# SyncE's list times set to those of a trace, and the stores of the split output weights given a later place

## The chip, the cores and the metric

The kernel runs on 1 core of one Trainium2 chip. The metric is the device time of one execution in microseconds. Three runs of the kernel before gave 1342.36, 1343.71 and 1345.11 us, median 1343.71.

## The reference

An attention without softmax feeds two feed-forward layers. B = 8 batches, H = 8 heads, S = 576 rows, D = 64, so 4608 tokens of 512 columns.

```python
kv = einsum('bhsd,bhse->bhde', k, v)
out = einsum('bhsd,bhde->bhse', q, kv)
out = out / sqrt(mean(out * out, axis=-1) + 1e-6) * g_norm
x = out.transpose(0, 2, 1, 3).reshape(4608, 512)
h = max(max(x @ w1, x @ w2), x @ w3)          # 512 -> 768
x = h @ w_out                                 # 768 -> 512
h = x @ w_in                                  # 512 -> 2048
g = s * relu(h)**2 + b
return g @ moe2_w_out                         # 2048 -> 512
```

## The kernel before

**Tiling.** The tokens are worked in nine blocks of 512. Blocks 0 to 7 are the first 512 rows of each batch; block 8 collects the 64 remaining rows of all batches. Weights and activations are split into a high and a low part, and a product is three matmuls (lines 183 to 185: high by high, high by low, low by high).

**Stages.** The first stage (every job whose position lies below CUT) does, in one stream: the attention of all batches (`load_kv`, `load_rem`, `load_q`, `q_turn`, `kv_mm`, `o_mm`, the norm in `o_sq`, `msc_mm`, `rsqrt_c`, `u_hi`, `u_both`, `wide_bc`, `normed`); the unpacking and splitting of the weights w1, w2, w3 (chunks w0 to w17) and w_out (chunks o0 to o5), in `plan_conv`; and the first layer of blocks 0, 1 and 2 by the plain way (`g1_part`, `g2_mm`). Later stages work the other blocks by a Strassen-like scheme with seven products in place of eight, and then the second layer.

**What goes through memory.** Normed attention outputs are stored to `xd` (`x_out`, lines 537 and 539). The results of the first layer's second product are copied out of PSUM on ScalarE (`g2_out`, L612) into a ring of two tiles (tag "st") and stored to `x1d` (`x1_store`, L615), by ScalarE's own DMA queue for blocks 0 and 1. The third copy of a block therefore waits until the first store has landed. A block's second product fills all four PSUM banks of the tag "g"; two of them then take the broadcast of a norm (`wide_bc`, L490), and the next block's `g1_part` waits for the bank of the third copy. The split output weights `W_o0` to `W_o5` (512 KB each) are stored to `od` (`wo_out`, L337) and come back only at the start of a later stage (`wo_back`, L1508, 530 to 549 us), because their slots are used for other things in between.

**Order.** No order is written out by hand. Each piece of work is a job with a position, an engine, a cost in us, what it reads and writes, and a lag from its end to when its result may be used. `arrange` (lines 73 to 153) plays these through and issues each engine's instructions in the order that comes out. At each step it takes the engine that can begin earliest and, of the jobs that are ready there, the first by position:

```python
begin, eng = min((max(free.get(e, 0.0), min(when(n) for n in h)), e) for e, h in heaps.items() if h)
n = min(m for m in heaps[eng] if when(m) <= begin)
```

So a cost shifts when later jobs count as ready, on every engine, and with it the order of the instructions; for jobs marked "DVE/ACT" it also decides which of the two engines takes them. A tag with so many slots makes a new tile's job wait for the last use of an old one. The chip then runs each engine's stream in that order with semaphores. Positions count in steps of one `g1` group; a block is SL = 22 of them, block 0 begins at 0, and CUT is 59.

**SyncE's jobs in the first stage.** Loads of k, v (one pair of heads at a time, two DMAs of 256 KB), of the remaining rows of k and v (two of 128 KB), of q (four DMAs of 288 KB into the one tile `qraw`, whose next load waits for the last `q_turn` of the one before), of the raw weights (512 KB), and the stores to `xd`, `od` and `wd`. The raw chunk o5 (and o4) is loaded into a slot that the unpacking of w14 (and w15) uses first; the first raw chunk of the second layer's weights (p0) goes into the tile "craw", which the unpacking of o4 uses last.

Of the kernel before, what the change touches and what calls it, by code (L numbers as in the profile page):

```python
# [30 lines left out]
def attention_max_ffn_relu2_ffn(ctx: ExitStack, tc, q, k, v, g_norm, w1, w2, w3, wo, wi, w2o, s, b, out):  # L31
# [14 lines left out]
    B, H, S, D = q.shape  # L46
# [13 lines left out]
    SL = G1 + KD  # L60
# [7 lines left out]
    def job(pos, eng, cost, fn, *args, r=(), w=(), a=(), lag=None):  # L68
        jobs.append((pos, len(jobs), eng, cost, fn, list(args), r, w, a, lag or (2.0 if eng == "SP" else 0.1)))
# [143 lines left out]
    od = dram.tile([P, M1, 2, N], F32, name="od")  # L213
# [99 lines left out]
    def stage(tag, name, shape, dtype):  # L313
        return lambda: (at_ if tag[0] == "c" else base).tile(shape, dtype, tag=tag, name=name, bufs=SIZE.get(tag, 1))
# [226 lines left out]
    def plan_x_out(bb, p, pos, o):  # L541
        if bb == B or p % 2:
            u = p if bb == B else p // 2
            job(pos, "SP", 1.1 if bb == B else 1.95, x_out, bb, u, r=o if bb == B else [f"o{bb}.{u}:0", f"o{bb}.{u}:1"],
                w=[f"xd{bb}:{c}" for c in ([2 * (p % 2) + p // 2] if bb == B else (u, 2 + u))])

    def x_tiles(j):
# [71 lines left out]
    def plan_conv(kk, src, pos, load, a, pr, slot=None, store=None):  # L619
        key = (kk[0], int(kk[1:]))  # L620
        raw, tr = f"raw_{kk}", f"tr_{kk}"
        ra, tra = stage(a, raw, [P, 4 * N], U16), stage(pr, tr, [P, 2, N], I32)
        gc = f"gc_{kk}"
        own = kk[0] != "p"
        gca = stage("cgc", gc, [P, N], U16) if own else lambda: st["tr", key][:, 1].bitcast(U16)[:, :N]
        job(load, "SP", 1.95, conv_load, key, src, ra, w=[raw], a=[(a, raw)], lag=6.0 if kk[0] == "p" else 2.0)
        job(pos, "DVE/ACT", (0.43, 0.66), conv_c, key, gca, None if own else tra, r=[raw], w=[gc if own else tr + ":r"],
            a=[("cgc", gc) if own else (pr, tr)])
        job(pos, "ACT", 0.71, conv_t, key, tra if own else None, r=[gc if own else tr + ":r"], w=[tr + ":t"], a=[(pr, tr)] if own else [])
        job(pos, "DVE/ACT", (0.43, 0.72), conv_r, key, r=[raw], w=[tr + ":r"])  # L630
        job(pos, "DVE", 0.69, conv_s, key, r=[raw], w=[tr + ":r"])
        job(pos, "DVE", 0.69, conv_sum, key, r=[tr + ":r"], w=[tr + ":t"])
        if store is None:
            job(pos, "ACT", 0.63, conv_hi, key, slot, r=[tr + ":t"], w=[f"W_{kk}:0"], a=[(slot, f"W_{kk}")])
            job(pos, "DVE", 0.69, conv_lo, key, r=[tr + ":t", f"W_{kk}:0"], w=[f"W_{kk}:1"])
        else:
            job(store, "SP", 1.1, conv_store, key, r=[tr + ":t"], w=[f"wd{key[1] // 4}:{key[1] % 4}"], lag=5 if pos < CUT else None)

    def plan_kv(bb, load, mm, n):
        lag = 2.0 if bb < 2 else 8.0  # L640
        job(load(0) + 0.01 if bb < 3 else mm(0) - WA + 0.1, "SP", 1.1, load_rem, bb, w=["rem"], lag=lag)
        for p in range(NP):
            job(load(p), "SP", 2.1, load_kv, bb, p, w=[f"k{bb}.{p}", f"v{bb}.{p}"],
                a=[("k", f"k{bb}.{p}"), ("v", f"v{bb}.{p}")], lag=lag)
            job(mm(p), "PE", 0.65, kv_mm, bb, p, r=[f"k{bb}.{p}", f"v{bb}.{p}", "rem"], w=[f"kvp:{p}"])
        for p in range(0, NP, n):
            job(mm(p + n - 1) + 0.01, "ACT", 0.4, kv_out, bb, p, n, r=[f"kvp:{i}" for i in range(p, p + n)],
                w=[f"kvc{bb}:{i}" for i in range(p, p + n)], a=[("kvc", f"kvc{bb}")] if p == 0 else [])
# [9 lines left out]
                w=[f"qh{bb}.{p // 2}:{p}"], a=[(HS[p // 2] if p < NP else "kvc", f"qh{bb}.{p // 2}")] if p % 2 == 0 else [])  # L658

    def plan_q(bb, p, n, pos):  # L660
        job(pos, "SP", 2.1 * n, load_q, bb, p, n, w=[f"qraw{bb}:{i}" for i in range(p, p + n)],
            a=[("qraw", f"qraw{bb}")] if p == 0 else [])

    def plan_o(bb, u, pp, turn, mm):
# [42 lines left out]
    def plan_wide(bb, t, f, sq):  # L707
        o = [[f"or{p}:{b_}" for b_ in range(B)] if bb == B else [f"o{bb}.{p // 2}:{p % 2}"] for p in range(NP)]
        ms, y, uc, uh, ul = (f"{c}c{bb}" for c in ("ms", "y", "u", "uh", "ul"))
        for p in range(NP):  # L710
            src, r = (lambda p=p: st["ops", p // 2][:, p % 2]), [f"ops{bb}.{p // 2}:{i}" for i in (p // 2 * 2, p // 2 * 2 + 1)]
            if bb == B:
                src, r = (lambda p=p: rest[0][:, p]), o[p]
            job(sq(p), "ACT", 0.59, lambda p=p, src=src: o_sq(bb, p, src()), r=r, w=[f"sq{bb}.{p}"], a=[(SQ[p], f"sq{bb}.{p}")])
        job(t, "PE", 1.1, msc_mm, bb, 0, NP, r=[f"sq{bb}.{p}" for p in range(NP)], w=[ms], a=[("ms", ms)])
        for i in range(5):
            job(t + f * (0.3 + 0.1 * i), "DVE" if i > 2 else "ACT", 0.7 if i > 2 else 0.65, rsqrt_c, bb, 0, NP, i,
                r=[[ms], [y], [y], [ms], [y]][i], w=[[y], [y], [uc], [uc], [uc]][i], a=[("y", y), ("u", uc)] if i == 0 else [])
        job(t + 0.9 * f, "DVE", 0.42, u_hi, bb, r=[uc], w=[uh], a=[("y", uh)])
        job(t + 1.0 * f, "DVE", 0.69, u_both, bb, r=[uc, uh], w=[ul], a=[("xb", ul)])  # L720
        b = [f"bc{bb}.0:0", f"bc{bb}.0:1", f"bc{bb}.1:0", f"bc{bb}.1x:0"]
        job(t + 1.3 * f, "PE", 0.52, wide_bc, bb, r=[ul], w=b, a=[("ops", f"bc{bb}.0"), ("*g", f"bc{bb}.1"), ("*g", f"bc{bb}.1x")])
        for k, p in enumerate((2, 3, 0, 1)):
            job(t + f * (1.6 + 0.05 * k), "DVE", 0.7, normed, bb, p, r=[b[p], "g_sb"], w=o[p])
            if bb == 1:
                plan_x(bb, p, 20 + 0.1 * p, o[p], "DVE", p == 0)
        for p in range(NP) if bb > 1 else ():
            plan_x_out(bb, p, t + f * (1.9 + 0.3 * (p // 2 * 2)), o[p])
# [41 lines left out]

    plan_q_rows(0, lambda p: Z - 0.5 + 0.1 * p, lambda p: Z - 0.1 + 0.02 * p if p < NP else Z - 0.12)
    plan_kv(0, lambda p: Z + p, lambda p: Z + p + 0.5, 1)
    job(Z + 2.45, "SP", 1.0, load_scalars, w=["scalars"])
    job(Z + 2.45, "DVE", 0.15, scale_g, r=["scalars"], w=["g_sb"])
# [10 lines left out]
    for n in range(G1):  # L785
        plan_conv(f"w{n}", w1_src(n), WS_ * n - 3 if n > 3 else Z + CP + n, WS_ * n - 5 if n > 3 else Z + LP[n], W1S[n], sets[n % 4], slot=W1S[n])
    for m in range(M1):
        plan_conv(f"o{m}", [(0, P, W16[3][m * P:(m + 1) * P, :])], WO_ + 0.8 * m, WO_ - 2 + 0.8 * m,
                  WOS[m], sets[m % 2], slot=WOS[m])

    for bb in range(1, B + 1):
# [9 lines left out]
        for u in range(NP // 2):  # L801
            a, f = (t + 6 * FA * u, FA) if bb > 1 else (A1 + AS * u, 1)
# [27 lines left out]
                    plan_g2(j, n, t + G1 + 0.3 + m * (0.5 if j == 0 else 0.66) + 0.01 * n, [m])  # L830
            plan_g2_out(j, n, t + G1 + (max(n + 1.01, 2.01 + 0.1 * n) if 0 < j < ND - 1 else 3 + 0.3 * n if j == 0 else 3.7 + 0.05 * n))
    for m in range(M1):
        job(SL + 6 + 3 * m, "SP", 1.95, wo_out, m, r=[f"W_o{m}:0", f"W_o{m}:1"], w=[f"od:{m}"])

# [673 lines left out]
    def plan_pairs():  # L1510
# [35 lines left out]
        for n in range(2 * M2):  # L1546
            if n < PA:
                pos, raw, pr = SL + 14 + (CUT - SL - 21) / PA * n, "craw", "ctr"
            elif n < PB:
                pos, raw, pr = TB + 28 + (TC - TB - 28 - 12) / (PB - PA) * (n - PA), *(("o2", "o3"), ("o4", "o5"))[n % 2]  # L1550
            else:
                pos, raw, pr = TC + 2 + 1.3 * (n - PB), *(("v0", "v1"), ("v2", "v3"))[n % 2]
            plan_conv(f"p{n}", p2_src(n), pos, pos - 3, raw, pr, store=pos + 1.5)
# [15 lines left out]
    for n, qq in enumerate(PAIRS):  # L1569
        for g in range(4):  # L1570
            for i in range(7):
                G = 4 * n + g
                pos = T2 + 7 * G + i
# [66 lines left out]
```

## Time and profile before

| | us |
|---|---|
| median of the runs | 1343.71 |
| the profiled execution, its own time | 1345.25 |
| its span | 1343.4 |
| TensorE (PE) busy | 1323.7 |
| VectorE (DVE) busy | 972.7 |
| ScalarE (ACT) busy | 765.3 |
| DMA queue of SyncE and its share of the 16 engines' span | 259.74 MB, 62.4% |
| share of PE in the chain that ended last | 95% |

The times are of one execution. Busy time leaves out DMA-issuing and semaphore instructions. The granted clock of TensorE is 0.998 of full speed over the span. A timeline row gives start, duration, engine, line, operation and output<-input; the bracket is the idle time of that engine ahead of it and what ended it. "SPq" and "ACTq" are the instructions by which SyncE and ScalarE issue DMAs.

### The profile page before, as it was taken

Reading aid. Unit: us, or ns where it says so; the run is one execution under the profiler, and the core shown is the slowest. Engines: PE = TensorE matmul, PEld = TensorE weight load, DVE = VectorE, ACT = ScalarE, POOL = GpSimd, SP = SyncE. Lnnn points to the kernel's source line nnn. Section 1 sums busy time; section 2 is a strip of 40 time slices with the busy share of each in tenths; the row PEclk is TensorE's granted clock in tenths of the full one; section 3 lists DMA queues with packets and bytes.
Section 4 is the critical chain, followed back from the end, with each engine's and each line's share of the span. In section 5 each row is a group of like instructions: output and inputs, shape, how many; then the busy total and the mean of one; then the engine's idle time right before and its main releaser. Section 6 shows DMA issues by size and latency. Waiting matters only on the chain.

```text
span 1343.4 us, 19629 instructions
## 1 busy us (share of the span) xinstructions
PE 1323.7 (99%) x6910; PEld 1083.4 (81%) x6910; DVE 972.7 (72%) x1677; ACT 765.3 (57%) x1360; POOL 16.9 (1%) x20
## 2 busy tenths in 40 slices
PE   7999998999999999999999999999999999999998
PEld 5776766788888888888888889888888888888888
DVE  5995455688977766665657668658888888888886
ACT  6874443464454643454656567567775757566565
POOL 0000100100000000000000000000000000000000
PEclk9999999999999999999999999999999999999999
DMA  9999998375458688775535655436584464453541
GB/s 279 292 193 255 222 220 189 123 248 206 180 195 254 189 256 275 250 245 184 180 142 189 233 184 176 167 134 224 195 310 149 145 206 151 162 176 123 188 125 59
DMA packets 245987, 264.41 MB, mean 197 GB/s; under 512 B 119680, under 2 KB 178560, under 8 KB 243712
## 3 DMA queue, kind: packets, MB, share of 16 engines
q1 hardware_dynamic: 244000, 259.74, 62.4%
q10 hardware_dynamic: 1888, 3.41, 0.8%
q8 instruction: 54, 0.88, 0.3%
q14 instruction: 45, 0.37, 0.1%
HBM read 159.29 MB, written 103.81 MB: 196 GB/s over the span
## 4 chain that ended last, share of the span: by engine, by line
PE 95%; DMA 2%; ACT 1%; SPq 1%; DVE 1%; issue 0%; ACTq 0%; DVEq 0%
PE ps_a L1015 15%; PE zs_a L1169 15%; PE fp_a L1444 11%; PE zs_b L1169 7%; PE ps_b L1015 7%; PE g L183 7%; PE g L185 7%; PE g L184 7%; PE fp_b L1444 5%; PE zs_c L1169 4%; PE ps_c L1015 4%; PE fp_c L1444 3%; PE kvor L382 1%; PE ops L451 1%; DMA x1d<-x 1%; PE msc L497 1%
## 5 line engine op out<-in xcount | busy, mean ns | idle before, releaser
L324 ACT ACTIVATE zx<-z 128x512 fp32r<-128x512 f32 (+1 forms) x280 | 158.5, 586 | 119.6 <-PE zs_a L1169 39.1
L1169 PE MATMUL zs_a<-zx,w_q 128*128 128x512 f32 (+1 forms) x960 | 211.0, 368 | 0.1
L327 DVE TENSOR_TENSOR zx<-z,zx 128x512 fp32r<-128x512 f32 (+1 forms) x280 | 171.7, 634 | 53.4 <-ACT zx L324 50.1
L1015 PE MATMUL ps_a<-x_q,w_q 128*128 128x512 f32 (+1 forms) x960 | 206.0, 368 | 0.0
L1169 PEld LDWEIGHTS zs_a<-zx,w_q 128*128 128x128 f32 x960 | 168.2, 188 | 30.3 <-DVE zx L327 0.3
L1015 PEld LDWEIGHTS ps_a<-x_q,w_q 128*128 128x128 f32 x960 | 167.8, 189 | 29.9
L1169 PE MATMUL zs_b<-zx,w_q 128*128 128x512 f32 (+1 forms) x480 | 108.6, 368 | 0.0
L1015 PE MATMUL ps_b<-x_q,w_q 128*128 128x512 f32 (+1 forms) x480 | 105.1, 368 | 0.0
L1169 PEld LDWEIGHTS zs_b<-zx,w_q 128*128 128x128 f32 x480 | 84.7, 189 | 15.1
L1015 PEld LDWEIGHTS ps_b<-x_q,w_q 128*128 128x128 f32 x480 | 84.2, 189 | 15.0
L183 PE MATMUL g<-xh,w_w 128*128 128x512 f32 x216 | 87.7, 406 | 2.8 <-ACT x L612 2.4
L185 PE MATMUL g<-xh,w_w 128*128 128x512 f32 x216 | 84.7, 392 | 0.7 <-DVE w_w L327 0.7
L184 PE MATMUL g<-xl,w_w 128*128 128x512 f32 x216 | 84.7, 392 | 0.2 <-DVE xl L327 0.2
L1452 ACT ACTIVATE fc<-fp_a 128x512 f32<-128x512 f32 x54 | 32.1, 596 | 69.3 <-PE fp_a L1444 63.7
L1044 ACT ACTIVATE cs<-cs 128x512 f32<-128x512 f32 (+1 forms) x60 | 35.1, 585 | 54.9 <-DVE cs L871 54.2
L1031 ACT ACTIVATE cs<-ps_a 128x512 f32<-128x512 f32 (+1 forms) x80 | 43.4, 554 | 26.1 <-PE ps_a L1015 22.3
L871 DVE TENSOR_TENSOR cs<-ps_b,cs 128x512 f32<-128x512 f32 (+1 forms) x40 | 24.9, 637 | 44.1 <-issue 32.9
L184 PE MATMUL g<-h,wo 128*128 128x512 f32 x144 | 56.1, 390 | 0.0
L185 PE MATMUL g<-h,wo 128*128 128x512 f32 x144 | 56.0, 389 | 0.0
L183 PE MATMUL g<-h,wo 128*128 128x512 f32 x144 | 56.0, 389 | 0.0
L183 PEld LDWEIGHTS g<-xh,w_w 128*128 128x128 f32 x216 | 40.5, 188 | 18.4 <-issue 5.6
L1169 PE MATMUL zs_c<-zx,w_q 128*128 128x512 f32 (+1 forms) x240 | 54.5, 368 | 0.0
(382 smaller groups left out, 2510.0 us busy)
## 6 DMA issues: line engine op xcount, KB each, us to landing
z<-gd SPq DMA_DIRECT2D x64, 512.0 KB
gd<-cs SPq DMA_DIRECT2D x96, 256.0 KB
fs<-sd SPq DMA_DIRECT2D x24, 512.0 KB
z<-gd SPq DMA_DIRECT2D x48, 256.0 KB
sd<-fs SPq DMA_DIRECT2D x18, 512.0 KB
hd<-fh SPq DMA_DIRECT2D x36, 256.0 KB
fhl<-hd SPq DMA_DIRECT2D x36, 256.0 KB
raw_w<-in_moe_w_dram SPq DMA_DIRECT2D x18, 511.0 KB
```

Source lines behind the costliest of these rows:

```text
L183: nc.tensor.matmul(ps, lhsT=w[:, 0, sl], rhs=xh, start=first, stop=False)
L184: nc.tensor.matmul(ps, lhsT=w[:, 0, sl], rhs=xl, start=False, stop=False)
L185: nc.tensor.matmul(ps, lhsT=w[:, 1, sl], rhs=xh, start=False, stop=last)
L324: act(out=out, in_=src, func=AF.Copy)
L327: eng.tensor_tensor(out=out, in0=src, in1=hi.bitcast(F32), op=ALU.subtract)
L871: eng.tensor_tensor(out=out, in0=in0, in1=in1, op=op)
L1015: nc.tensor.matmul(ps, lhsT=w[:, a, c], rhs=x[:, b_], start=new and k == 0 and e == 0, stop=k == HK - 1 and e == 2, skip_group_check=True)
L1031: act(out=st["cs", G, i, m], in_=st["ps", G, BANK[i], m][:, :n], func=AF.Copy)
L1044: act(out=h, in_=st["ps", G, BANK[i], m][:, :width(q)] if i == 6 else h, func=AF.Relu)
L1169: nc.tensor.matmul(ps, lhsT=w[:, a, c], rhs=x[:, b_], start=new and k_ == 0 and e == 0, stop=k_ == 3 and e == 2, skip_group_check=True)
L1444: nc.tensor.matmul(ps, lhsT=w[:, u, c], rhs=x[:, v_], start=new and k == 0 and e == 0, stop=k == HK - 1 and e == 2, skip_group_check=True)
L1452: act(out=st["fc", a, G, i], in_=ps, func=AF.Copy)
```

## The change

Seven numbers change, all of them positions or costs that `arrange` reads; no instruction is added or taken away, and no other line is touched.

```diff
     def plan_x_out(bb, p, pos, o):
-            job(pos, "SP", 1.1 if bb == B else 1.95, x_out, ...
+            job(pos, "SP", 0.75 if bb == B else 1.4, x_out, ...
...
     def plan_conv(kk, src, pos, load, a, pr, slot=None, store=None):
-        job(load, "SP", 1.95, conv_load, ...
+        job(load, "SP", 1.95 if kk[0] == "p" else 1.75, conv_load, ...
...
     def plan_kv(bb, load, mm, n):
-            job(load(p), "SP", 2.1, load_kv, ...
+            job(load(p), "SP", 1.75, load_kv, ...
...
     def plan_q(bb, p, n, pos):
-        job(pos, "SP", 2.1 * n, load_q, ...
+        job(pos, "SP", 2.95 * n, load_q, ...
...
     for m in range(M1):
-        job(SL + 6 + 3 * m, "SP", 1.95, wo_out, m, ...
+        job(2 * SL + 4 + 1.8 * m, "SP", 1.4, wo_out, m, ...
```

With n = 4, the list's time of a load of q goes from 8.4 to 11.8 us. The six stores of the split output weights go from the positions 28, 31, 34, 37, 40, 43 to 48, 49.8, 51.6, 53.4, 55.2, 57; block 2 spans the positions 44 to 66.

## Rows read from the trace of the kernel before

**Rows 1.** Page, view 1: busy us (share of the span) and number of instructions.
```profile
PE 1323.7 (99%) x6910; PEld 1083.4 (81%) x6910; DVE 972.7 (72%) x1677; ACT 765.3 (57%) x1360; POOL 16.9 (1%) x20
```
**Rows 2.** Stretches: length, busy us (x) of PE, PEld, DVE, ACT, POOL, clock, DMA share, GB/s.
```profile
40.00:50.00 10.00, 10.00 (x62) 8.07 (x61) 9.27 (x16) 5.34 (x10) 0.00 (x0) 1.00 1.24 230
...
100.00:110.00 10.00, 9.63 (x119) 7.56 (x121) 2.72 (x4) 2.39 (x4) 0.00 (x0) 1.00 0.93 342
...
200.00:210.00 10.00, 5.50 (x24) 3.55 (x22) 5.72 (x9) 1.19 (x2) 0.00 (x0) 0.97 1.03 351
```
**Rows 3.** The same view, first and last of seven stretches from 280 to 1330 us.
```profile
280.00:400.00 120.00, 120.00 (x531) 99.38 (x530) 102.06 (x181) 62.27 (x106) 0.00 (x0) 1.00 0.55 196
...
1200.00:1330.00 130.00, 129.93 (x710) 113.32 (x709) 108.46 (x208) 82.87 (x167) 0.67 (x2) 1.00 0.41 133
```
**Rows 4.** Waits of PE over the span: total us, times, longest us.
```profile
PE bc L490 <- DVE ul L482: 2.7, 2, 2.1
PE g L183 <- ACT x L612: 2.4, 1, 2.4
```
**Rows 5.** Waits of PE from 100 to 135 us.
```profile
PE bc L490 <- DVE ul L482: 0.7, 1, 0.7
...
PE g L183 <- ACT xh L324: 0.4, 1, 0.4
PE g L184 <- DVE xl L327: 0.2, 1, 0.2
```
**Rows 6.** Timeline of SyncE's issues, 58 to 108 us.
```profile
58.83 0.38 SPq L370 DMA_DIRECT2D v<-in_v_dram  x1
71.22 2.84 SPq L271 DMA_DIRECT2D raw_o<-in_moe_w_out_dram  x2
...
96.88 0.89 SPq L337 DMA_DIRECT2D od<-w_o  x2
...
98.50 1.00 SPq L337 DMA_DIRECT2D od<-w_o  x1
107.03 0.38 SPq L370 DMA_DIRECT2D k<-in_k_dram  x1
```
**Rows 7.** Timeline of SyncE's issues, 126 to 221 us.
```profile
126.41 0.47 SPq L337 DMA_DIRECT2D od<-w_o  x1
...
220.13 3.51 SPq L337 DMA_DIRECT2D od<-w_o  x1
```
**Rows 8.** Chain that ended last, 103 to 111 us: start us, us, what.
```profile
103.89 4.07 DMA x1d<-x
...
108.05 0.61 ACT x L612
...
110.11 0.64 ACT xh L324
```
**Rows 9.** The same chain, 197 to 208 us.
```profile
197.30 4.01 DMA k<-in_k_dram
...
201.39 6.30 DMA x1d<-x
```
**Rows 10.** Timeline of DVE and ACT, 95 to 208 us.
```profile
95.88 0.68 DVE L327 TENSOR_TENSOR w_o<-tr_o,w_o 128x512 fp32r<-128x512 f32 x1
...
128.39 0.78 DVE L438 STREAM_TRANSPOSE qt<-qraw 128x576 f32<-128x576 f32 x1 [2.50 <-DMA qraw<-in_q_dram]
...
199.21 0.78 DVE L438 STREAM_TRANSPOSE qt<-qraw 128x576 f32<-128x576 f32 x1 [6.91 <-DMA qraw<-in_q_dram]
...
207.67 0.60 ACT L612 ACTIVATE x<-g 128x512 f32<-128x512 f32 x1 [11.27 <-DMA x1d<-x]
```
**Rows 11.** Stretches of 2 to 6 us: columns as in rows 2.
```profile
65.00:71.00 6.00, 6.00 (x28) 4.98 (x27) 6.00 (x11) 5.99 (x11) 0.00 (x0) 1.00 0.32 111
...
104.00:106.00 2.00, 2.00 (x13) 1.41 (x11) 0.00 (x0) 0.60 (x1) 0.00 (x0) 1.00 1.05 418
...
208.00:210.00 2.00, 1.68 (x6) 1.18 (x6) 0.00 (x0) 0.87 (x2) 0.00 (x0) 0.84 1.05 404
210.00:212.00 2.00, 2.00 (x9) 0.55 (x12) 0.00 (x0) 0.00 (x0) 0.00 (x0) 0.50 0.95 337
212.00:214.00 2.00, 2.00 (x60) 1.79 (x54) 1.40 (x3) 1.61 (x3) 0.00 (x0) 0.81 0.08 32
```

More of the change, by code (lines that the diff above doesn't have):

```diff
@@ L543, in plan_x_out @@
             u = p if bb == B else p // 2
-            job(pos, "SP", 1.1 if bb == B else 1.95, x_out, bb, u, r=o if bb == B else [f"o{bb}.{u}:0", f"o{bb}.{u}:1"],
+            job(pos, "SP", 0.75 if bb == B else 1.4, x_out, bb, u, r=o if bb == B else [f"o{bb}.{u}:0", f"o{bb}.{u}:1"],
                 w=[f"xd{bb}:{c}" for c in ([2 * (p % 2) + p // 2] if bb == B else (u, 2 + u))])
@@ L625, in plan_conv @@
         gca = stage("cgc", gc, [P, N], U16) if own else lambda: st["tr", key][:, 1].bitcast(U16)[:, :N]
-        job(load, "SP", 1.95, conv_load, key, src, ra, w=[raw], a=[(a, raw)], lag=6.0 if kk[0] == "p" else 2.0)
+        job(load, "SP", 1.95 if kk[0] == "p" else 1.75, conv_load, key, src, ra, w=[raw], a=[(a, raw)], lag=6.0 if kk[0] == "p" else 2.0)
         job(pos, "DVE/ACT", (0.43, 0.66), conv_c, key, gca, None if own else tra, r=[raw], w=[gc if own else tr + ":r"],
@@ L642, in plan_kv @@
         for p in range(NP):
-            job(load(p), "SP", 2.1, load_kv, bb, p, w=[f"k{bb}.{p}", f"v{bb}.{p}"],
+            job(load(p), "SP", 1.75, load_kv, bb, p, w=[f"k{bb}.{p}", f"v{bb}.{p}"],
                 a=[("k", f"k{bb}.{p}"), ("v", f"v{bb}.{p}")], lag=lag)
@@ L660, in plan_q @@
     def plan_q(bb, p, n, pos):
-        job(pos, "SP", 2.1 * n, load_q, bb, p, n, w=[f"qraw{bb}:{i}" for i in range(p, p + n)],
+        job(pos, "SP", 2.95 * n, load_q, bb, p, n, w=[f"qraw{bb}:{i}" for i in range(p, p + n)],
             a=[("qraw", f"qraw{bb}")] if p == 0 else [])
@@ L832, in attention_max_ffn_relu2_ffn @@
     for m in range(M1):
-        job(SL + 6 + 3 * m, "SP", 1.95, wo_out, m, r=[f"W_o{m}:0", f"W_o{m}:1"], w=[f"od:{m}"])
+        job(2 * SL + 4 + 1.8 * m, "SP", 1.4, wo_out, m, r=[f"W_o{m}:0", f"W_o{m}:1"], w=[f"od:{m}"])
     p2 = {}
```

## The prediction

> **What bounds the kernel now.** I read the busy times first, then the stretches, then TensorE's waits, and last the chain of waits and the timelines where PE stands. PE is busy for 1323.7 of 1343.4 us [rows 1], and the loss is not spread out. From 280 to 1330 us PE is busy throughout, in seven stretches of which the first and the last stand in [rows 3]; from 40 to 100 us it is busy for 10.00 of every 10 us (six stretches, the first in [rows 2]). What the change can give back inside the stage that it reorders lies in two places: 100 to 132 us (waits of 0.7, 0.4 and 0.2 us [rows 5]) and the end of block 1 (5.50 of 10 us busy from 200 to 210 [rows 2]). The latter is two waits, 2.06 us (the "2.1" of the row) for the broadcast L490 on VectorE's L482, and 2.4 us for g L183 on ScalarE's copy L612 [rows 4]. After them the granted clock stood at 0.84, 0.50 (its lower level, 1.2 of 2.4 GHz) and 0.81 over three times 2 us [rows 11]; at 2 us each that is (0.16 + 0.50 + 0.19) x 2 = 1.7 us lost. So the prize is at most 4.5 + 1.7 + 1.3 = 7.5 us, 0.6% of the time, and everything else in the stage can only get worse.
>
> The 4.5 us have two causes in a row. VectorE stood 6.91 us, until 199.21, in front of a transpose of q that waits for its load, and the norm's steps were queued behind it [rows 10]; that made the first wait. ScalarE stood from 196.40 to 207.67 in front of the third copy of block 1, for the landing of a store to x1d [rows 10]. The chain goes through this second one alone: a load of k landed at 197.30 + 4.01 = 201.31, the store was let go then and took 6.30 us for 256 KB [rows 9].
>
> **The change, part by part.** No instruction is added or taken away, so everything is order. The sum is made against the profiled execution, 1345.25 us.
>
> *Place of the six stores.* A position is a rank and not a time. The loop takes, for the engine that is free first, the lowest ready job, and it never leaves an engine idle for a job that isn't ready. The stores at positions 28, 31 and 34 were issued at 96.88 (two) and 98.50 [rows 6], in block 0, whose positions end at 22, because SyncE had nothing else until the k load at 107.03. That gap stays: the next loads of k wait for PE's products of the block before. Now SyncE reaches it earlier by the list's own costs: the 18 + 6 raw chunks are 0.20 each shorter, sixteen pairs of k and v up to there 0.35 each, and two loads of q 3.4 each longer: 4.8 + 5.6 - 6.8 = 3.6 us earlier. The gap, at least 7.8 us long (three stores and p0 at 1.95 were put there), becomes some 11, into which the raw load p0 (now ahead of them by rank) at 1.95 and six stores at 1.4, 10.35 in all, just fit. All six splits are done by then: the last low part ends at 95.88 + 0.68 [rows 10]. I expect five or six of the stores there, ahead of block 1, and none or one at the end of block 2. What goes from 126.41 and 220.13 [rows 7] frees nothing that PE waits for: 0, with ends of -0.3 and 0.
>
> *What three more stores do at 97 to 104 us.* The store of x1d that was issued at 103.89 landed 4.07 us later, behind those already queued [rows 8], and DMA moved 418 GB/s with its engines full [rows 11]. Three more stores are 1.57 MB, at that rate 3.8 us. Behind the landing stand, on ScalarE, the copies at 108.05 and 109.11 and then xh at 110.11 [rows 8], and PE's first product of block 1 waits for that. ScalarE has 0.5 us of slack in between, so the upper end is +3.4 us. The lower end is -0.6, if the store lands no later and the waits of 0.4 and 0.2 us [rows 5] go. Against the upper end stands this: SyncE did nothing from 59.21 to 71.22 because the raw chunk o5 stood ahead in its queue [rows 6], and DMA was at 0.32 of its share from 65 to 71 [rows 11]. In the new list SyncE comes to that point 3.8 us earlier (18 and 4 chunks, eight pairs, one q: 4.4 + 2.8 - 3.4), when o5's slot is not free, so loads of block 2's k and v pass it and fill this hole; that takes up to 1.3 MB out of the later queue, 3 us at 418 GB/s. The two nearly cancel: 3.8 - 3.0 - 0.5 of slack gives about +0.3, and I take +0.5.
>
> The store of x1d goes by ScalarE's queue, the others by SyncE's. The Trainium skill, in "DMA: Bandwidth & Descriptors", section "Queues, rings and completion order", says that a DMA engine serves its queues in turn, packet by packet; by that alone more stores on the other queue would cost next to nothing, and the term would be 0. The same section says that a completion is written only after every earlier write of that engine, across its queues, which would give the 3.8. The trace sides with the second: 6.30 us for 256 KB with a long queue and 4.07 with a short one [rows 8, 9].
>
> *q at 11.8 us in place of 8.4.* The list now counts the transposes as ready 3.4 us later after a q load begins, so on VectorE they go behind the norm's last steps (L513 to L482). At 128.39 VectorE waited 2.50 us for q and PE 0.65 for what came after [rows 5, 10]: -0.65, with ends of -0.7 and 0. At 199.21 the same happens and PE's 2.06 us go, but then PE comes to the second wait 2.06 us sooner and that grows from 2.4 to some 4.5, because the store's landing at 201.39 + 6.30 = 207.69 [rows 9] does not move: the loads ahead of it are the same ones. That is 0; a pair of k and v that slips ahead of q there may let it land earlier by its 0.5 MB at 404 GB/s [rows 11], 1.3 us. I take -0.4 between -6.2 (both waits and the clock go: 4.5 + 1.7) and +1.3 (the same 0.5 MB falls behind and the store lands later).
>
> *The weights' unpacking from 20 to 100 us.* Ready times move by 1 to 4 us, so VectorE and ScalarE swap some pieces. Both are busy there, PE never waits from 40 on [rows 2]; 0, with ends of -1 and +2.
>
> Sum: 0 + 0.5 - 0.65 - 0.4 + 0 = -0.55, so 1344.7 for an execution like the profiled one. That one was 1.54 above the median of the runs, so the median to expect is 1343.2.
>
> **The rivals.** *R1, the stores pile up ahead of block 0's results (slower).* All six are queued between 95 and 102 us and the hole at 59 to 71 stays empty, so x1d lands at 111.8, PE stands 3.4 us more at 111, and as after the stand at 203 to 208 the clock drops for 1.7. With -0.65 that is +4.45: 1348.2, or 1346.5 without the clock. It decides once the landing passes 108.5. For it: DMA is full from 98 on [rows 2, 11]; against it, the hole.
> *R2, the end of block 1 heals (faster).* The store to x1d is let go at 196.40, when ScalarE gets there, because what it waits for is an earlier transfer than that k load, or fewer loads of k and v stand ahead. Then it lands before PE needs the bank, 4.5 us ahead of 208.3, and 4.5 + 1.7 + 0.65 go: -6.85, 1336.9; half of it is 1340.3. For it: the longer q pushes k and v back in the list. Against it: q has the lower position there and its rank doesn't change, so the same loads follow it and are queued when ScalarE comes to the store.
> *R3, the stores do go to the end of block 2*, so the three early ones leave: 3.8 us less queue ahead of x1d, the waits of 0.4, 0.4 and 0.2 us at 109 to 112 go, with 0.65: -1.6, 1342.1.
> *R4, a weight comes late* in block 0 through the new order on VectorE: +2 and more, 1346.
>
> **How the numbers follow.** No change is within 0.2% here, 2.7 us, about what a measurement of this kernel can tell. The forecast has 0.40, R1 0.16, R2 0.29, R3 0.08, R4 0.07. R2's full size lies beyond 1338 and R1 with the clock beyond 1348; the range from 1338.2 to 1347.4 leaves out about one in ten on either side. Beside it, the forecast's own range is 1341.5 to 1345.5. Faster: R2 and 0.04 of the forecast, 0.33. Slower: R1 and R4, 0.23. Same: the rest, 0.44.
>
> **What would show it.** In the trace of the changed kernel: L337 five or six times between 95 and 103 us (R3: after 200); k and v of block 2 issued between 59 and 71; the landing of x1d near 108 (R1: 110 or later); no wait of VectorE for q over 1 us; L490 without a wait; one wait of some 4 to 5 us of L183 on L612 near 208 with a dip of the clock after it. The forecast is wrong if PE's busy share from 200 to 210 rises above 8 of 10, or if a wait of over 2 us stands anywhere before 132.

## The result and the profile after

The changed kernel took 1351.33 us (median of 6 runs, 1349.17 to 1353.63) against 1343.7 for the kernel before on the same chip (6 runs, 1342.36 to 1348.44): ratio 1.0051, interval 1.0033 to 1.0069. It is slower, by 7.6 us, and lies outside the predicted range. The profiled execution took 1353.63 us with a span of 1351.4, 8.0 more than before.

The page after, busy times, answers to [rows 1]: TensorE (PE) has the same 6910 instructions and is busy 4.4 us longer. So about half of the 8 us is idle time; the other half is busy time, and the table below shows that it was spent at a lower clock.

```profile
PE 1328.1 (98%) x6910; PEld 1086.7 (80%) x6910; DVE 978.0 (72%) x1682; ACT 762.7 (56%) x1355; POOL 17.0 (1%) x20
```

The stretches after answer to [rows 2] and [rows 3] (length, busy us of PE, PEld, DVE, ACT, POOL, granted clock, DMA share, GB/s):

```profile
20.00:30.00 10.00, 4.88 (x42) 2.43 (x44) 6.53 (x14) 7.08 (x13) 0.00 (x0) 0.79 1.11 265
30.00:40.00 10.00, 9.77 (x58) 5.50 (x58) 6.26 (x11) 7.90 (x13) 0.00 (x0) 0.53 1.19 288
40.00:50.00 10.00, 10.00 (x60) 7.23 (x59) 9.44 (x16) 6.85 (x13) 0.00 (x0) 1.00 1.14 166
...
110.00:120.00 10.00, 7.71 (x116) 5.56 (x114) 2.72 (x4) 3.39 (x7) 0.00 (x0) 1.00 1.02 375
120.00:130.00 10.00, 9.66 (x44) 6.88 (x45) 6.85 (x13) 6.99 (x13) 0.00 (x0) 0.83 1.05 215
200.00:210.00 10.00, 8.65 (x86) 5.93 (x79) 1.76 (x5) 6.13 (x11) 0.00 (x0) 1.00 1.29 169
...
280.00:400.00 120.00, 119.87 (x530) 98.95 (x529) 105.44 (x186) 64.75 (x109) 0.00 (x0) 1.00 0.59 213
1200.00:1330.00 130.00, 129.93 (x679) 111.99 (x678) 108.66 (x199) 83.01 (x161) 0.66 (x2) 1.00 0.45 142
```

Before, the first two of these stretches, which the prediction did not look at, were:

```profile
20.00:30.00 10.00, 8.42 (x74) 4.46 (x71) 8.12 (x16) 9.85 (x18) 0.00 (x0) 1.00 0.90 283
30.00:40.00 10.00, 9.28 (x72) 6.22 (x71) 9.40 (x16) 9.92 (x17) 0.00 (x0) 1.00 1.13 263
```

From 20 to 30 us TensorE's busy time fell from 8.42 to 4.88, and the clock was below full in both stretches: at the lower of its two levels (0.50) for some (0.21 + 0.47) x 10 x 2 = 13.6 us. From 110 to 130 a second loss came, with a second dip; from 200 to 210 some was won (5.50 in [rows 2], 8.65 now). From 280 on next to nothing changed (119.87 of 120 us busy, before 120.00).

TensorE's waits after, over the span, answer to [rows 4]: both waits of before are gone, and four others of over 1.3 us have come. (A wait of some 5 us for the first load of q, at the very start, stands in both kernels.)

```profile
PE kvor L382 <- DMA v<-in_v_dram: 4.3, 2, 4.1
PE g L183 <- ACT xh L324: 2.4, 1, 2.4
PE ops L451 <- ACT o L461: 1.6, 1, 1.6
PE kvor L382 <- DVE o_rem L474: 1.4, 1, 1.4
```

Where the first stands is seen in the timeline of PE after,

```profile
21.65 1.05 PE L497 MATMUL msc<-sq,means 128*32 128x512 f32 x4
...
27.90 1.12 PE L382 MATMUL kvor<-v,k 128*64 128x64 f32 x16 [4.08 <-DMA v<-in_v_dram]
29.54 0.48 PE L382 MATMUL kvor<-vrem,krem 128*64 128x64 f32 x4 [0.52 <-DMA vrem<-in_v_dram]
...
31.81 2.08 PE L526 MATMUL bc<-uc,spread 32*128 32x512 f32 x4
```

and in the timeline of PE before.

```profile
18.34 1.53 PE L497 MATMUL msc<-sq,means 128*32 128x512 f32 x4 [0.77 <-ACT sq L468]
...
23.96 1.13 PE L526 MATMUL bc<-uc,spread 32*128 32x512 f32 x4 [0.22 <-DVE uc L515]
25.63 1.52 PE L497 MATMUL msc<-sq,means 128*32 128x512 f32 x4 [0.54 <-ACT sq L468]
27.08 0.69 PE L382 MATMUL kvor<-v,k 128*64 128x64 f32 x16
```

Two things moved. Block 1's first product of k and v (L382) now stands ahead of the broadcast of block 0's norm (L526). And the norm's first matmul (L497) runs 3.3 us later, since two more products of block 0's own k and v (16.41 and 18.64) went ahead of it. The broadcast's input, the result of L515 on VectorE, is ready at 23.22 + 0.68 = 23.90 us before and at 27.68 + 0.68 = 28.36 us after; most of these 4.5 us come from the later start of L497. In VectorE's timelines, before and after:

```profile
23.22 0.68 DVE L515 SCALAR_TENSOR_TENSOR uc<-uc,yc 64x512 f32<-64x512 f32 x1
```

```profile
27.68 0.68 DVE L515 SCALAR_TENSOR_TENSOR uc<-uc,yc 64x512 f32<-64x512 f32 x1
```

So there was nothing of the norm that TensorE could have done in the 4.08 us. It does keep to the order of its stream: at 29.02 it stood 0.52 us more, for the remaining rows of v, with the broadcast's input ready. The chain after gives the load that it waits for:

```profile
17.89 9.88 DMA v<-in_v_dram
```

The list counts such a pair as usable 1.75 + 2.0 = 3.75 us after its start (before: 4.1); it landed 9.88 us after its issue, at 27.77. It was later than the list's time before too: by the trace's semaphore records the v load of that pair, issued at 16.82, landed at 23.99, 7.2 us later, but its product came only at 27.08.

To compare the kernels with one measure I add up, from stretches of 2 us, TensorE's idle time and, for the low clock, its busy time times (1 - clock). What this leaves out is the pace of TensorE's work at full clock, which differs between the orders too (see e8 and e14). A cell is idle + clock, in us:

| kernel | 0-20 | 20-45 | 45-100 | 100-130 | 130-180 | 180-230 | 230-340 | sum |
|---|---|---|---|---|---|---|---|---|
| before | 6.4 | 2.3 | 0 | 1.6 | 0 | 4.5+1.6 | 0 | 16.4 |
| after | 7.1 | 5.3+5.4 | 0 | 2.6+1.6 | 0 | 2.9 | 0.1 | 25.2 |
| e3, place alone | 7.0 | 2.3 | 0 | 2.6+1.7 | 0 | 4.9+1.7 | 1.3 | 21.5 |
| e4, k and v alone | 8.0 | 4.7+2.9 | 0 | 1.5 | 1.0 | 3.2+1.6 | 0 | 22.8 |
| e5, place, held | 8.4 | 2.3 | 0 | 1.5 | 0.5 | 6.8+1.6 | 1.1 | 22.1 |
| e6, after, held | 7.8 | 3.8+4.8 | 0 | 0 | 0 | 2.0 | 0.4 | 18.6 |
| e7, e6 with early k, v back | 7.3 | 2.0 | 1.3 | 0 | 0 | 3.2 | 0.1 | 13.9 |
| e9, e7 with q back | 8.5 | 1.5+1.7 | 0 | 1.1 | 2.4+3.2 | 5.0 | 0.1 | 23.4 |

After minus before is +9.1 up to 45 us, +2.6 from 100 to 130 and -3.2 from 180 to 230, in all 8.8 with the roundings, for a span that is 8.0 longer.

The stores after, in SyncE's timeline, answer to [rows 6] and [rows 7]: five at once ahead of block 1, one at 162.19, none at the end of block 2.

```profile
63.51 0.61 SPq L365 DMA_DIRECT2D krem<-in_k_dram  x1
64.96 1.90 SPq L365 DMA_DIRECT2D vrem<-in_v_dram  x1
76.94 0.35 SPq L271 DMA_DIRECT2D raw_o<-in_moe_w_out_dram  x1
...
104.06 3.78 SPq L337 DMA_DIRECT2D od<-w_o  x5
...
162.19 0.43 SPq L337 DMA_DIRECT2D od<-w_o  x1
```

ScalarE's timeline after, at the results of block 0, answers to [rows 8]: the first store to x1d was issued at 110.72 and let the third copy go at 117.34, 6.6 us later (before: 103.89 to 108.05, 4.2). TensorE then lost 2.4 us for xh and some 1.6 to the clock.

```profile
110.72 0.35 ACTq L615 DMA_DIRECT2D x1d<-x  x1
...
117.34 0.60 ACT L612 ACTIVATE x<-g 128x512 f32<-128x512 f32 x1 [5.30 <-DMA x1d<-x]
```

The DMA queues after show that the store's data themselves came late. From 110 to 114 us only SyncE's queue (q1) moved anything, and from 114 to 118 both did (packets, MB, share of the engines). Queue q10 is ScalarE's: in e6 below it alone moved from 109 to 110 us, 0.26 MB, with one store of 256 KB under way.

```profile
q1 hardware_dynamic: 461, 1.68, 102.8%
```

```profile
q1 hardware_dynamic: 528, 0.97, 66.0%
q10 hardware_dynamic: 288, 0.52, 35.7%
```

### The profile page after: what moved, and what is told of

The parts are those of the page before. It is cut to its first block, busy times and chain, and to the rows that moved or that the text cites. A ratio compares the mean times of both kernels' runs of the same rounds, so it can differ in the third digit from the quotient of the medians.

```text
span 1351.4 us, 19617 instructions
## 1 busy us (share of the span) xinstructions
PE 1328.1 (98%) x6910; PEld 1086.7 (80%) x6910; DVE 978.0 (72%) x1682; ACT 762.7 (56%) x1355; POOL 17.0 (1%) x20
## 4 chain that ended last, share of the span: by engine, by line
PE 94%; DMA 3%; DVE 1%; SPq 1%; ACT 0%; issue 0%; ACTq 0%; DVEq 0%
PE ps_a L1015 15%; PE zs_a L1169 15%; PE fp_a L1444 11%; PE zs_b L1169 7%; PE ps_b L1015 7%; PE g L183 7%; PE g L184 7%; PE g L185 7%; PE fp_b L1444 5%; PE zs_c L1169 4%; PE ps_c L1015 4%; PE fp_c L1444 3%; DMA v<-in_v_dram 2%; PE kvor L382 1%; PE ops L451 1%; DMA xl<-xd 1%
## 5 line engine op out<-in xcount | busy, mean ns | idle before, releaser
L327 DVE TENSOR_TENSOR zx<-z,zx 128x512 fp32r<-128x512 f32 (+1 forms) x280 | 171.8, 634 | 53.4 <-ACT zx L324 50.1
```

Source lines behind the costliest of these rows:

```text
L327: eng.tensor_tensor(out=out, in0=src, in1=hi.bitcast(F32), op=ALU.subtract)
```

## The experiments

The theories: T1, the new count of k and v puts TensorE's products at the start in another order, and it stands there; T2, the stores that are bunched ahead of block 0's results delay their landing; T3, q's count. They were joined by T5, that any order of SyncE's queue but the one before opens waits of some us somewhere, and T6, that q's count matters because a longer one puts the turning of q behind the norm's last steps on VectorE. Each was timed beside the kernel before on the same chip, where that had medians from 1343.9 to 1344.3; the runs are spread over four chips, so ratios compare them better than medians.

| run | what | median us | ratio to before, interval |
|---|---|---|---|
| e1 | after, k and v of blocks 0, 1 at 2.1 | 1348.72 | 1.0040, 1.0028 to 1.0053 |
| e2 | after, longer lag for block 1 | 1352.81 | 1.0071, 1.0058 to 1.0084 |
| e3 | before, stores' place and count | 1351.51 | 1.0059, 1.0046 to 1.0071 |
| e4 | before, k and v at 1.75 | 1349.79 | 1.0043, 1.0029 to 1.0056 |
| e5 | e3, stores held behind block 1 | 1353.27 | 1.0060, 1.0048 to 1.0073 |
| e6 | after, stores held behind block 1 | 1346.87 | 1.0021, 1.0010 to 1.0033 |
| e7 | e6 with e1's edit | 1343.83 | 0.9993, 0.9983 to 1.0003 |
| e8 | before, q at 11.8 | 1357.77 | 1.0094, 1.0080 to 1.0108 |
| e9 | e7, q at 8.4 | 1350.74 | 1.0043, 1.0030 to 1.0055 |
| e10 | after, each store issued twice | 1359.10 | 1.0105, 1.0092 to 1.0119 |
| e11 | before, stores held behind block 0 | 1352.34 | 1.0064, 1.0050 to 1.0077 |
| e12 | e7, weights at 1.95 | 1348.95 | 1.0031, 1.0019 to 1.0043 |
| e13 | e7, x_out at 1.95 and 1.1 | 1347.14 | 1.0022, 1.0010 to 1.0034 |
| e14 | e7, all k and v at 2.1 | 1348.83 | 1.0033, 1.0022 to 1.0043 |
| e15 | e7, q at 10.6 | 1346.29 | 1.0007, 0.9996 to 1.0019 |

**e1, e2: the start mended in two ways, in the changed kernel.**

```diff
-            job(load(p), "SP", 1.75, load_kv, ...
+            job(load(p), "SP", 2.1 if bb < 2 else 1.75, load_kv, ...      # e1
...
-        lag = 2.0 if bb < 2 else 8.0
+        lag = 8.0 if bb else 2.0                                          # e2
```

> The changed kernel, but k and v of batches 0 and 1 count as 2.1 us again (later batches 1.75). By the list, PE then does the broadcast of batch 0's norm before batch 1's k by v product again, and four stores of the split output weights still stand ahead of block 0's results. T1 (the loss is the order at 18 to 40 us, which comes from the 1.75 of the first k and v): no wait of 4 us at 24, clock at full there, 1343 to 1346. T2 (the loss is the stores ahead of block 0's results): it stays, 1348 to 1351. T3 (the longer q is to blame): also stays at 1348 or more.

> The changed kernel with every cost and place of the change, but the list lets the loads of batch 1's k and v be used 8 us after their end and not 2 us. By the list PE's product of batch 1 moves behind the broadcast of batch 0's norm. T1: the wait at 24 us goes although k and v still count 1.75, and 6 to 7 us of time with it: 1343 to 1346; what is left over the kernel before is the wait of some 2.4 us for xh at 120 us and its clock, as five stores are still there. T2 and T3: 1349 to 1352, as nothing that they name is touched.

e1: the stop at 27.9 us and the low clock behind it are gone (loss up to 45 us 9.6 instead of 17.8), but the time fell only to 1348.72, and its interval overlaps that of the changed kernel: T1 alone does not carry it. e2 missed: it moves block 1's product behind the broadcast, but L497 stays late (21.27 us), so TensorE stood 2.94 us at 26.38 for the norm itself, and 3.23 us at 198.67. So the late norm is a part of the loss at the start, beside the late load.

**e3, e4: single edits in the kernel before.** e3 takes the line of `wo_out` alone, e4 the 1.75 of `load_kv` alone.

> The kernel before with the six stores alone changed (place and 1.4 us). By the list four of them go into the gap ahead of block 0's results in place of three, two some 25 us later, none to the end of block 2. T1: within 2 us of the kernel before, 1342 to 1345.5. T2: one more store of 0.5 MB in the queue, a landing later by 1.3 us, and a wait for xh of up to 2 us with a dip of the clock: 1345 to 1347.

> The kernel before with the cost of k and v loads alone at 1.75. By the list batch 1's product goes ahead of batch 0's broadcast, as in the changed kernel, and five stores fit into the gap. T1: the wait of 4 us at 24 us, the clock at half to 39 us, 1349 to 1352. T2: only as much as the stores bring, 1345 to 1347. T3: 1343 to 1345, since q stays at 8.4.

e4 came as T1 said (L497 at 21.46), and showed the same stop in the timeline of PE:

```profile
26.95 0.76 PE L382 MATMUL kvor<-v,k 128*64 128x64 f32 x16 [3.32 <-DMA v<-in_v_dram]
```

This stop is in each of the four kernels that count early k and v at 1.75 with the old lag (after, e4, e6, e10: 4.1, 3.3, 2.8 and 1.3 us, in e10 with a second one of 2.2), and in none of the twelve that count them at 2.1 (before, e1, e3, e5, e7 to e9, e11 to e15). e3 came out above every expectation: the place alone costs as much as the whole change. Its three waits of PE were these.

```profile
113.14 0.49 PE L183 MATMUL g<-xh,w_w 128*128 128x512 f32 x1 [1.98 <-ACT xh L324]
192.21 1.21 PE L451 MATMUL ops<-qt,kvc 64*64 64x512 f32 x8 [2.80 <-ACT o L461]
211.47 0.50 PE L490 MATMUL bc<-ul,spread 32*128 32x512 f32 x4 [2.11 <-DVE ul L482]
```

The first is T2's, with four stores ahead of the results instead of three; the other two belong to the end of block 1.

**e5, e6, e7: the stores held back.** A seventh edit, one more key that a store reads, keeps all six behind block 1's result; e5 is e3 with it, e6 the changed kernel, e7 the changed kernel with e1's edit too.

```diff
-        job(2 * SL + 4 + 1.8 * m, "SP", 1.4, wo_out, m, r=[f"W_o{m}:0", f"W_o{m}:1"], ...
+        job(2 * SL + 4 + 1.8 * m, "SP", 1.4, wo_out, m, r=[f"W_o{m}:0", f"W_o{m}:1", "x1d1:3"], ...
```

> The kernel before with the stores' new position and count alone, and one more key among what a store reads: the last quarter of block 1's result, so that the list can place none of the six before that is stored (by the list all six then stand at 215 to 234 us, none ahead of block 0's results). T2 (what the position costs is that four stores, not three, stand ahead of block 0's results, which land later: in the run with the position alone TensorE lost 2.0 us to that at 113 us and 1.7 us to the half clock behind it): the loss at 113 us is gone, 1343 to 1346 us. T5 (any order of SyncE's queue other than that of before opens waits of some us at the ends of blocks 0 and 1, wherever the stores are): 1347 to 1352 us.

> The changed kernel with the same key: none of the six stores can stand before block 1's result. T1 and T2 together (the start costs some 7 us and stays; the wait for block 0's results at 120 us, 2.4 us and 1.7 us of half clock, goes): 1346.5 to 1349 us, with the stop at 27.9 us and the half clock behind it unchanged. T5: 1350 us or more, the loss only moved.

> The changed kernel with k and v of the first two blocks counted at 2.1 again, and the same key on the stores. T1 and T2 (both losses away): 1342 to 1346 us, with no half clock before 200 us. T5: 1347 to 1351 us, since e1 lost its time in several small waits and not in one.

e6 and e7 came as T1 and T2 said. In e6 block 0's results flow without a wait for a landing; the third copy waits for nothing but PE, in ScalarE's timeline:

```profile
108.33 0.35 ACTq L615 DMA_DIRECT2D x1d<-x  x1
...
110.84 0.60 ACT L612 ACTIVATE x<-g 128x512 f32<-128x512 f32 x1 [1.18 <-PE bc L490]
```

The stop at the start stayed in e6 (2.75 us, then 4.8 us lost to the clock). e7 is level with the kernel before. So in the changed kernel the two causes together are the whole loss: 1351.3 to 1346.9 by holding the stores, to 1343.8 by the old count of early k and v. Undone in the other order (e1, then e7) the count is worth 2.6 and the stores 4.9 us; by the ratios, and over both orders, the stores are worth 4.0 to 6.3 us and the count 1.5 to 3.8. T3 is out as a cause of the loss, since e7 keeps q at 11.8.

e5 fell to T5: TensorE lost nothing to block 0's results, but stood 6.82 us at 210.61 for the norm of batch 4. The timelines of SyncE, ScalarE, VectorE and PE:

```profile
198.76 0.64 SPq L365 DMA_DIRECT2D vrem<-in_v_dram  x1
...
204.06 0.33 ACTq L615 DMA_DIRECT2D x1d<-x  x1
204.44 0.69 ACT L507 ACTIVATE yc<-msc,eps 128x512 f32<-128x512 f32 x1 [10.33 <-DMA vrem<-in_v_dram]
...
206.82 0.69 DVE L513 SCALAR_TENSOR_TENSOR uc<-msc,uc 128x512 f32<-128x512 f32 x1 [14.65 <-ACT uc L511]
...
210.61 0.80 PE L490 MATMUL bc<-ul,spread 32*128 32x512 f32 x4 [6.82 <-DVE ul L482]
```

The norm was late because ScalarE was. It had copied the first of block 1's results by 194.11, but issued its store only at 204.06, 10.0 us later, and the norm's steps L507 to L511 stood behind that issue. What the issue waited for is a load of the remaining rows of v, which landed at 203.99: by the trace, the store uses the same completion semaphore as that load, and ScalarE first waits for it. With q at 8.4 two transposes of q (L438, 0.77 us each) also stand among the norm's steps on VectorE, but VectorE did not wait for q here.

**e8, e9, e15: q's count.** e8 is the kernel before with 2.95 * n; e9 and e15 are e7 with 2.1 * n and 2.65 * n.

> The kernel before with q's load counted at 11.8 us instead of 8.4 and nothing else: by the list the stores then stand at 113, 115, 144, 215, 241 and 248 us. The prediction's term for q (VectorE's waits for q go, -0.65 us at 128 and -0.4 us at 200 us): 1342 to 1344 us. T5: 1347 to 1352 us. T2: two stores ahead of block 0's results instead of three, so no loss at 113 us.

> The kernel of e7 (the changed one with k and v of blocks 0 and 1 at 2.1 and the stores held behind block 1's result) with q's load counted at 8.4 us again. The prediction's term for q (11.8 is worth 1.05 us): 1344 to 1346 us. T6 (with 8.4 the q of block 5 is issued so late that VectorE stands at its turning ahead of block 4's scale at the end of block 1, as in e5, where TensorE lost 6.8 us at 210 us): 1348 to 1352 us, with a wait for ul of some us near 205 us.

> The kernel of e7 with q's load counted at 10.6 us, between the old 8.4 and the new 11.8. T6 (what counts is that VectorE's turning of q comes behind the norm's last steps in the order): if 10.6 is late enough for that at both ends of block 1, 1342 to 1345 us; if not, a wait for ul at 130 or at 200 us as with 8.4, and 1347 to 1351 us.

e9 is the clean one. Without the changed count, e7 loses 6.9 us. VectorE's timeline in e9,

```profile
123.83 0.69 DVE L515 SCALAR_TENSOR_TENSOR uc<-uc,yc 128x512 f32<-128x512 f32 x1
129.84 0.78 DVE L438 STREAM_TRANSPOSE qt<-qraw 128x576 f32<-128x576 f32 x1 [5.32 <-DMA qraw<-in_q_dram]
130.54 0.38 DVE L478 TENSOR_SCALAR uh<-uc 128x512 fp32r<-128x512 f32 x1
```

against e7's, where the norm goes on at once:

```profile
125.70 0.69 DVE L515 SCALAR_TENSOR_TENSOR uc<-uc,yc 128x512 f32<-128x512 f32 x1
126.43 1.40 DVE L478 TENSOR_SCALAR uh<-uc 128x512 fp32r<-128x512 f32 x1
127.86 0.75 DVE L482 SCALAR_TENSOR_TENSOR ul<-uh,more,uc 128x512 fp32r<-128x512 f32 x1
```

In e9 PE stood 3.02 us at 132.29 and lost 3.2 to the clock behind it. That is T6's mechanism, though at 130 us and not at 205 where its expectation had it, and not in e5, from which it was taken. e15 shows that 10.6 is long enough at 130 us (no wait for ul there); PE stood 3.81 us at 196.30 for VectorE's o_rem instead, and the time, between the two ranges expected, is not told from that of before. e8 missed by far: by itself in the old order the new count of q costs 13.6 us. TensorE had no wait for block 0's results, as T2 said, but 2.4 us of wait for a split weight at 58.66 and 3.8 for the norm at 269.58, each with the clock behind it; some 6.7 of the 13.1 us of its longer span do not show as TensorE's idle time or clock before 340 us. Most of that is busy time at full clock: by the page TensorE is busy for 1330.9 us in e8 and 1323.7 before, and without the clock terms (3.2 and 1.6) for 1327.7 and 1322.1, with the same 6910 instructions. Which of them ran at a slower pace was not found.

**e10: the stores' bytes.** The order and all counts are those of the changed kernel; each store is followed by a second one to a spare buffer.

```diff
     def wo_out(m):
         nc.sync.dma_start(out=od[:, m], in_=wt["o", m].bitcast(F32))
+        nc.sync.dma_start(out=od2[:, m], in_=wt["o", m].bitcast(F32))
```

> The changed kernel, its order and counts untouched, but every store of a split output weight is issued twice, the second time to a spare buffer that nobody reads, so ten transfers of 512 KB instead of five stand ahead of block 0's results. T2 (what delays block 0's results is the bytes of the stores that share the DMA engines with them): ScalarE's wait for the first result's landing grows from 5.3 us to 9 us or more, and the kernel to 1354 to 1359 us. T2b (it is only the order of the other work that the list changed with them): the wait stays at 5 to 6 us and the time at 1350 to 1352.5 us.

ScalarE's timeline of e10 (L614 is L612 of the others):

```profile
108.72 0.60 ACT L614 ACTIVATE x<-g 128x512 f32<-128x512 f32 x1 [6.41 <-PE g L185]
112.59 0.35 ACTq L617 DMA_DIRECT2D x1d<-x  x1
113.00 0.60 ACT L614 ACTIVATE x<-g 128x512 f32<-128x512 f32 x1 [3.67 <-DMA od<-w_o]
...
119.20 0.60 ACT L614 ACTIVATE x<-g 128x512 f32<-128x512 f32 x1 [5.61 <-DMA x1d<-x]
```

TensorE then stood 6.50 us for xh, and the kernel took 7.8 us more than the changed one, just past the upper end of what T2 said. But T2's sign, a wait of 9 us for the first landing, came only as a sum of two different waits, 3.67 + 5.61 = 9.3. The 3.67 us are in front of the issue of the first store. By the trace ScalarE waits there until 112.51 for a completion semaphore that SyncE's store of 103.95 used before, so the queue delays that store and the store delays ScalarE. From its issue to its landing the first result took 6.5 us (112.59 to 119.12), no more than in the changed kernel (110.72 to 117.26). T2b, the order of the other work alone, does not explain 7.8 us more in an order that did not change.

What holds of T2 is a delay by what SyncE's queue moves in the meantime. By the packets and semaphores of the traces, the first result took 2.4 us from issue to landing where that queue moved nothing (the nine runs with no store ahead, e6 among them), 4.1 us with 0.8 MB (before), and 6.5 us with 2.1 MB (after) and with 2.3 MB (e10).

**e11: the same in the kernel before.** Its stores keep position and count, with "x1d0:3" as the further key.

> The kernel before with its own counts, its stores at their old position but held behind the last of block 0's results, so that none of the three stands ahead of them (by the list at 131, 133, 135, 183, 213 and 225 us). T2 alone: ScalarE's wait of 2.83 us at 108 us goes, and with it the 1.6 us that TensorE lost between 100 and 130 us: 1341 to 1343 us. T5 (with the old counts any other order opens a wait at the end of block 1): 1346 to 1352 us.

The wait of 2.83 us on ScalarE went (0.72 was left), as T2 said, but that was worth 0.5 us to TensorE, and the new order stood at the end of block 1, as in e5, with ScalarE's store again held for 8.2 us until a load of the remaining rows of v had landed:

```profile
207.06 0.80 PE L490 MATMUL bc<-ul,spread 32*128 32x512 f32 x4 [5.17 <-DVE ul L482]
```

**e12, e13, e14: the other counts, each put back in e7** (1.95 for all raw weights; 1.95 and 1.1 for `x_out`; 2.1 for all k and v).

> The kernel of e7 with the weights' loads counted at 1.95 us again. It lost 1.3 us between 45 and 100 us, 0.98 us of them in a wait for a split weight at 58 us, which the kernel before didn't. If the lower count for the weights is the cause, the wait goes and the time is 1341.5 to 1343.5 us, below the kernel before; if not, 1343.5 us or more.

> The kernel of e7 with the stores of attention outputs and of block 8 (x_out) counted at 1.95 and 1.1 us again. The prediction gave them no term: 1343 to 1344.7 us. T5 (any count that moves SyncE's order opens a wait): 1346 us or more.

> The kernel of e7 with the loads of k and v counted at 2.1 us for all blocks, so not for 0 and 1 alone. What is left of the change is q, the weights' and results' counts and the held stores. If the later blocks' count has no part in the gain that q's brings, 1343 to 1345 us; T5: 1346 us or more, with the wait at the end of block 1 back.

Each costs 3 to 5 us against the kernel before (ratios 1.0022 to 1.0033). In e12 the expected gain did not come: the wait for a split weight near 58 us grew from 0.98 to 2.41, and one of 1.63 us came at 104.29. In e13 PE stood 2.74 us at 189.91, with the clock behind it. e14's idle and clock terms up to 340 us, 15.3, are below those of before; it loses by pace, as e8 does: without the clock term TensorE is busy for 1325.7 us against 1322.1. No version beats the kernel before by more than can be measured. T5 as a law is refuted by e7; as a count it stands: of the fifteen orders other than that of before (the change and all experiments but e10, which has the change's), two (e7, e15) are not told from it and none is faster.

One way in which an order opens such waits can be read from the traces. The program's DMAs take their completion semaphores in turn, across both queues, and a store's issue waits until the earlier user of its semaphore has landed; the order decides which transfer that is. For the first store of block 1's results the issue came 5.9 us after the copy's end in the kernel before, 7.1 in e3, 10.0 in e5, 8.2 in e11, 0.7 in the changed kernel, and at once in e7 and e12 to e14. No run changes the semaphores alone, so what this is worth by itself is not shown, and e12 to e14 lose without it.

## Why the prediction was wrong

**Two terms of the sum failed: the last one, "The weights' unpacking from 20 to 100 us", 0 with ends of -1 and +2, by its mechanism, and the one for the stores, +0.5, by its size.** The last one argued from VectorE and ScalarE and from the stretches after 40 us. From 20 to 40 TensorE is not busy throughout, and its own jobs are ordered by the same ready times: 0.35 us off the count of k and v was enough to put two products ahead of the norm's first matmul and another ahead of the broadcast. The norm's result came 4.5 us later and the load 3.8 us later (28.36 and 27.77, before 23.90 and 23.99), and TensorE stood. It cost 9.1 us up to 45 us in the trace, of which 5.4 are the clock. That the cause is this count is shown by e1, e4 and e7. What the median loses by it is less, 3.0 us (e6 against e7): e6 had lost 7.1 more than e7 by 45 us, then 1.3 less up to 100 and 1.2 less at the end of block 1, and TensorE's busy time without the clock term is 3.2 us shorter in e6; the two profiled spans differ by 1.7. Why a late start is partly made good was not tested.

**The place of the stores** was right: five in the gap ahead of block 1 and one later, none at the end of block 2, though at 104 us since all was late by some 7.

**What more stores do there** was sized wrong: +0.5 was said, 2.6 came in the trace (with 1.6 of clock, and net of the 0.65 that q's count took away at 130), and 4.5 in the median by e6. In time this is the larger of the two misses. R1 had the mechanism, with +3.4 and a clock drop of 1.7; I let the hole at 59 to 71 us argue it down. The hole was filled in part, as said (loads of block 2 from 60.61 to 66.9), but SyncE still stood from there to 76.94 ahead of o5, and eight loads of block 3's k and v were issued right ahead of the stores, from 98.97 to 103.5. The queue that x1d meets was no shorter. The store's landing took 6.5 us instead of 4.1. The prediction chose between two sentences of the Trainium skill, "DMA: Bandwidth & Descriptors", section "Queues, rings and completion order": that a DMA engine takes its queues in turn by packets, and that a completion is written after every earlier write of the engine. The runs do not settle that choice. A delay came, so the term of 0 drawn from the first does not hold; but it began ahead of the store's own data, whose first packet moved 3.4 us after the issue (0.85 in e6), and not between the data and the completion alone, as the second would have it.

**q at 11.8** went in the right direction. VectorE no longer stands for q ahead of the norm, and both waits of [rows 4] are gone; the end of block 1 lost 2.9 us in place of 6.1, -3.2 where -0.4 was taken (R2's half). That q's count alone did this is not shown. The second wait went as R2 has it: ScalarE's store was let go 0.7 us after its copy instead of 5.9, because the transfer whose semaphore it waits for was now an earlier one, a load of q; the prediction had held that the landing does not move. What q's count is worth in the new order, 6.9 us by e9, was far above the term of 1.05: without it TensorE stood 3.02 us at 132 and lost 3.2 to the clock, where before it had lost 0.65.

So terms of 0, +0.5 and -1.05 stood for +9.1, +2.6 and -3.2 us in the traces. The prediction's own signs of being wrong both came: a wait of over 2 us before 132 twice (4.1 at 27.9 and 2.4 at 120, besides the one at the very start that both kernels have), and a busy share of 8.65 of 10 from 200 to 210. The terms also do not add: the parts alone cost 7.6 (e3), 5.9 (e4) and 13.6 us (e8), and all together 7.6.

## What to carry to other kernels

When a cost in a list scheduler changes, replay the order of every engine, the bounding one first, from the first instruction on, and look for an instruction that now stands ahead of the work that used to cover its load, or ahead of a step that later work waits for: the true landing (9.88 us here against 3.75 in the list) decides, not whether the count came nearer to the trace. Look also at what the issue of a store waits for: here it was often a load that has nothing to do with it. Counting one quantity right can be worse than counting several wrong in balance: undoing one of the other counts in e7 cost 3 to 7 us each time. Stores that can wait should be tied behind the results that can't, by what they depend on and not by a rank, for a rank lets them into the first gap.

## What was not expected of the hardware

The low clock around a stop lasted very differently. With stops of 2.4 us (before at 208, after at 120) it cost some 1.6 us. With the stop of 4.1 us at 27.9 in the changed kernel the clock stood at 0.50 for some 13.6 us, 2 of them inside the stop, and after the stop TensorE had only two short gaps in that time (0.5 and 0.2 us). With the longest stop, 6.82 us in e5, it stood there for some 6.8 us, but more than half of that lay inside the stop, so it again cost 1.6.

What looked at first like one engine's queue holding up another's (the first store in e10, by 3.3 us, and in e5, by 10.0) is in the program and not in the queues: ScalarE runs a wait for a completion semaphore that a transfer of SyncE's used before.
